# GpSimd's and the transfer queue's orders kept as written in the rounds that make w_down's operands, and these operands asked for behind the last part of x

## The chip, the cores and the metric

The kernel runs on one core of a Trainium2 chip. The core has five engines with an instruction stream each: TensorE (PE in the profile, with its weight loads as PEld), VectorE (DVE), ScalarE (ACT), GpSimd (POOL) and SyncE (SP). SP computes nothing here: it issues every transfer between the device memory and the on-chip buffers, one behind the other, and where a transfer has to wait for something, SP waits, and all that stands behind it waits too. The metric is the device time of one execution in microseconds (us); lower is better.

## The reference

A layer norm feeds two branches that are multiplied at the end: attention with 32 heads of 18 columns, and a gated feed-forward net.

```python
def reference(A_x, A_wqkv, A_wo, B_x, B_w_gate, B_w_up, B_w_down):
    def _A_ref(x, wqkv, wo):
        ...
        scores = jnp.einsum("bhqd,bhkd->bhqk", q, k) * (Dh ** -0.5)
        p = _softmax(scores, axis=-1)
        o = jnp.einsum("bhqk,bhkd->bhqd", p, v)
        return (lambda x, *d: x.transpose(*d))(o, 0, 2, 1, 3).reshape(B, S, D) @ wo
    def _B_ref(x, w_gate, w_up, w_down):
        return (_gelu(x @ w_gate) * (x @ w_up)) @ w_down
    xn = _layernorm(A_x, axis=-1)
    s = _A_ref(xn, A_wqkv, A_wo)
    g = _silu(_B_ref(xn, B_w_gate, B_w_up, B_w_down))
    return A_x + s * g
```

There are 2048 tokens of 576 columns in float32, and the feed-forward net is 4608 wide. Products run in a 22-bit format (`F32R`); so every operand is split into a high and a low part, and three products stand for one.

## The kernel before

**Sections and rounds.** Behind a prologue (layer norm, projections) the work is a row of 144 *sections*. A section takes one block of 512 tokens (there are four, `NB`) and one slab of 128 hidden columns: 27 pairs of matmuls into `pg` and `pu` (gate and up), the activation into a tile `t`, and its split into `ah` and `al`. Two sections make a *round* (`G = 2`): at its end the slab of `w_down` for these 256 columns is there, and the product of the round, "downs" in the code, is added into `Y` on TensorE in the section after, behind its gate-and-up pairs. 18 rounds make a token block. In sections 10 to 137 the attention is woven into the gate-and-up pairs: `pm` is a score product for the row maxima, `pe` one for the exponentials, `acc` the product with the values, which stands at the end of every odd section. One group of four heads and 512 queries (a *unit*, `u`) takes four sections; its maxima have to stand in rows of the tiles `q` (by the way `m2t`, `mT`, `q<-mT`) before its first `pe`.

**The rounds in question.** Rounds 23 to 67 (`SEVEN`) form the product with w_down with seven block products in place of eight. They need sums of blocks of w_down as split operands, `BH` and `BL` (`bh`, `bl` in the profile). These are made once, in the 18 rounds before (`PREP`, rounds 5 to 22, sections 10 to 45), and kept in device memory as `ds` (one tensor a round; the tensor that is made for round 4 of a block is read again for round 4 of the others). In such a round:

- `load_down` (L774) brings the slab of w_down into `TY`; at the round's end it is split into `bh`, `bl` on GpSimd (L119 and L121), where the ordinary product reads it.
- in the first section of the next round `cut_differences` (L713) makes four differences in `TY` (L718), and splits them: the high part goes into a buffer called `raw`, the low part stays in `TY`.
- in the second section of that round `stores` (L722 to L726) writes `ds`: two pieces of `bh`, two of `bl`, all of `raw`, all of `TY`. Only then is `TY` free for the next `load_down`.

The buffer `raw` has two copies (L131). They serve the weights of gate and up of the next section (`load_gu`, L134) and that high part in turn. From `raw` GpSimd makes `wh` and `wl`, three pieces of each in a section (`split_gu`, L142); the pieces of the next section are made while this one runs.

In the rounds of `SEVEN`, `load_seven` (L730) reads `bh` and `bl` back from `ds` at the end of the round's second section. At the end of a token block `load_xd_part` (L150) loads the next block's transposed x in three parts of two tiles (`xd`), and GpSimd copies each to the other 64 partitions.

**What sets the order.** TensorE's order is the order in which the code is written. For the other engines and for SP's queue a scheduler orders the instructions, except where the code calls `tc.keep_in_program_order` on an instruction: these stay in the order of the code among themselves. `kept` (L516) does that only towards the end of the kernel. `no_sync(a, b, why)` puts a behind b in the order without a wait. The functions take a parameter (`keep`, `pin`) that says which of the two holds.

In the attention's loop (the last lines printed below) one turn asks first for the stores of K (`store_k`, `kx<-Km`), then runs a section (weights, `ds` stores and w_down in it), then asks for the next K (`load_k`: `Ks<-kx`, and `Km<-qk` in six pieces), the queries and maxima, and in odd sections the values (`load_v`, `VS`).

Of the kernel before, what the change touches and what calls it, by code (L numbers as in the profile page):

```python
# [17 lines left out]
P = 128  # L18
NT = S // P
TB = 512  # L20
# [60 lines left out]
def kernel(ctx: ExitStack, tc: tile.TileContext, x, wqkv, wo, w_gate, w_up, w_down, out):  # L81
# [36 lines left out]
    def split(hi, lo, raw, keep=lambda i: i):  # L118
# [3 lines left out]
        return first  # L122

    def split_ap(hi, lo, raw):
        tc.keep_in_program_order(nc.scalar.activation(hi, raw, AF.Copy))
        nc.gpsimd.tensor_tensor(lo, raw, f(hi), op=ALU.subtract)
# [22 lines left out]

    def load_xd_part(b, xd, c, keep=lambda i: i):  # L150

        for i in range(2):
            t = wts.tile([P, XG, TB], F32R, name=f"xd{i}_{c}")
            asked[:] = [nc.sync.dma_start(f(t)[0:HR], xhs[b][i, c * HR:(c + XG) * HR, :].rearrange("(k p) t -> p k t", p=HR))]
            keep(nc.gpsimd.tensor_copy(t[HR:P], t[0:HR]))  # L155
            xd[i].append(t)
# [556 lines left out]
    def cut_differences(r, raw):  # L713

        raw = raw.rearrange("p g (c n) -> p (g c) n", c=2)
        b11, b12, b21, b22 = range(4)
        for to, x, y in ((b11, b12, b11), (b12, b22, b12), (b22, b22, b11), (b21, b22, b21)):
            keep(nc.gpsimd.tensor_tensor(raw[:, to], raw[:, x], raw[:, y], op=ALU.subtract))  # L718
        high, low = raw_wide().rearrange("p (s n) -> p s n", s=4).bitcast(F32R), raw.bitcast(F32R)
        split(high, low, raw, keep)  # L720

        def stores():  # L722
            for i, (four, t) in enumerate(((BH, high), (BL, low))):
                nc.sync.dma_start(ds[r][i, :, B11, :], f(four)[:, b11, :])
                nc.sync.dma_start(ds[r][i, :, B21:B22 + 1, :], f(four)[:, b21:b22 + 1, :])
                nc.sync.dma_start(ds[r][i, :, T1:T2 + 1, :], f(t))  # L726

        FF["stores"].append(stores)

    def load_seven(r):  # L730
        for i, t in enumerate((BH, BL)):
            nc.sync.dma_start(f(t), ds[r][i])

# [39 lines left out]

    def load_down(r, raw):  # L774
        kept(nc.sync.dma_start(raw, w_down[r * G * P:(r + 1) * G * P, :].rearrange("(g p) n -> p g n", p=P)))
        return raw

    def section(specials=(), tag="f", raw_d=None, ahead=True):
# [20 lines left out]
        if g == G - 1 and not seven(n):  # L799
            FF["rawd"] = FF.pop("first_d") if n < G else load_down(  # L800
                r, raw_d() if raw_d else down_pair(TY) if n // G in PREP else raw_wide().rearrange("p (g n) -> p g n", g=G)) \
# [17 lines left out]
        def x_part(k):  # L819
            if new_x:  # L820
                load_xd_part(b + 1, xd, XG * k, tc.keep_in_program_order)

# [4 lines left out]
        if nxt and ahead:  # L827
            split_gu(nxt, NG - 1, pin)
        FF["w"] = nxt
# [23 lines left out]
    def finish(pool=ffn, cut=split):  # L853
# [66 lines left out]
    with tc.tile_pool(name="att", bufs=1, reuse_waits="tile") as att:  # L920
# [43 lines left out]

        def load_v(n):

            u, c = divmod(n, NA)
            if u < NU:
                g = u % NQ
                nc.sync.dma_start(VS[n % VB][:, 0:VC * VW].rearrange("p (t x) -> p t x", x=VW),  # L970
                                  vs[c * TB:(c + 1) * TB, QD * g:QD * (g + 1), :].rearrange("(t p) h d -> p t (h d)", p=P))

# [399 lines left out]
```

## Time and profile before

| | |
|---|---|
| time, median of 3 runs (lowest to highest) | 2692.07 us (2683.3 to 2692.53) |
| the profiled execution | 2687.61 us |
| its span, first to last instruction | 2685.8 us |
| mean granted TensorE clock | 0.978 |
| PE busy | 2572.2 us (96%) |
| DVE, POOL, ACT busy | 2072.8, 1724.0, 1578.4 us |
| moved by the queue of SP | 516.74 MB in 456992 packets |
| chain that ended last | PE 78%, POOL 8%, DMA 7%, DVE 3% |

The span is what the trace shows; 1.8 us of the execution lie outside it. "Busy" of PE counts slowly clocked matmuls in full, so 96% does not mean that TensorE could not be faster: a stretch has to be compared with another stretch of the same work. In the 40 slices of the page each slice is 67 us; the rounds of `PREP` lie in slices 5 to 16.

### The profile page before, as it was taken

What the parts mean: (1) busy time and instruction counts of PE and PEld (TensorE: products, weight loads), DVE (VectorE), ACT (ScalarE), POOL (GpSimd) and SP (SyncE); (2) the same over time, 40 slices, a digit from 0 to 9 for tenths busy, and PEclk for the clock granted to TensorE, in tenths of its full rate; (3) what the DMA queues carried; (4) which work ended last, traced back from release to release, by engine and by line L of the source; (5) the groups of instructions that cost most, each with busy time, mean ns of one, the idle gap of its engine ahead of it and who ended that gap; (6) DMA issues with size and microseconds to landing.
All of it is one profiled execution on the core that took longest, in us unless ns stands there. A gap on an engine that the chain in (4) does not pass through costs nothing.

```text
span 2685.8 us, 59575 instructions
## 1 busy us (share of the span) xinstructions
PE 2572.2 (96%) x21766; PEld 1963.5 (73%) x21766; DVE 2072.8 (77%) x3621; ACT 1578.4 (59%) x3009; POOL 1724.0 (64%) x2031
## 2 busy tenths in 40 slices
PE   9999989888988999999999999999999999999999
PEld 8889867575665767777776777777776777777788
DVE  5218867575766767899998899999998999999277
ACT  3223555454555555677776677777666676666722
POOL 3137656555556766666666866666667866666785
PEclk9999999898998999999999999999999999999999
DMA  7877555666667667767668766666768766666584
GB/s 248 276 248 186 153 173 174 183 180 177 188 174 215 204 177 207 195 189 193 187 188 210 207 189 191 192 187 189 194 192 210 205 189 194 191 192 180 142 241 141
DMA packets 457284, 520.55 MB, mean 194 GB/s; under 512 B 117776, under 2 KB 314416, under 8 KB 456992
## 3 DMA queue, kind: packets, MB, share of 16 engines
q1 hardware_dynamic: 456992, 516.74, 67.7%
q8 instruction: 174, 2.85, 0.5%
q14 instruction: 118, 0.97, 0.1%
HBM read 407.95 MB, written 108.64 MB: 192 GB/s over the span
## 4 chain that ended last, share of the span: by engine, by line
PE 78%; POOL 8%; DMA 7%; DVE 3%; issue 2%; SPq 2%; ACT 0%; POOLq 0%; ACTq 0%; DVEq 0%
PE pg L532 24%; PE acc L1083 12%; PE py L670 9%; PE pm L995 8%; PE pe L1048 7%; PE po L194 6%; PE pu L532 5%; PE py L600 4%; PE po L1232 2%; POOL wl L121 2%; DMA ds<-TY 2%; DVE mx L998 1%; POOL TY L718 1%; DMA raw<-in_B_w_up_dram 1%; POOL TY L121 1%
## 5 line engine op out<-in xcount | busy, mean ns | idle before, releaser
L1049 ACT ACTIVATE pT<-pe 128x512 f32<-128x512 f32 x2048 | 1155.8, 599 | 570.3 <-PE pm L995 297.3
L998 DVE TENSOR_REDUCE mx<-pm 128x1 f32<-128x512 f32 x2048 | 1266.9, 682 | 265.8 <-PE pm L995 197.3
L532 PE MATMUL pu<-xd,wh 64*128 64x512 f32 x2592 | 953.0, 400 | 15.1 <-POOL xd L155 14.5
L532 PE MATMUL pg<-xd,wh 64*128 64x512 f32 x2592 | 952.5, 400 | 8.2 <-POOL wh L119 5.0
L1048 PE MATMUL pe<-q,Ks 64*128 64x512 f32 x2048 | 797.4, 398 | 22.1 <-DMA q<-mT 15.3
L995 PE MATMUL pm<-Km,q 64*128 64x512 f32 x2048 | 800.9, 398 | 1.3 <-DVE accs L1088 0.8
L532 PEld LDWEIGHTS pg<-xd,wh 64*128 64x128 f32 x2592 | 489.1, 189 | 139.7 <-POOL ah L119 26.2
L532 PE MATMUL pg<-xd,wl 64*128 64x512 f32 x1296 | 516.5, 399 | 59.3 <-POOL wl L121 59.3
L121 POOL TENSOR_TENSOR wl<-raw,wh 128x384 fp32r<-128x384 f32 x432 | 444.1, 1029 | 176.2 <-PE pu L532 156.6
L532 PE MATMUL pu<-xd,wl 64*128 64x512 f32 x1296 | 516.1, 398 | 0.0
L532 PEld LDWEIGHTS pu<-xd,wh 64*128 64x128 f32 x2592 | 489.6, 189 | 28.3 <-POOL xd L155 17.8
L1083 PE MATMUL acc<-pT,VS 128*32 128x512 f32 x4096 | 452.8, 594 | 0.0
L1048 PEld LDWEIGHTS pe<-q,Ks 64*128 64x128 f32 x2048 | 381.6, 190 | 57.8 <-DMA q<-mT 17.3
L995 PEld LDWEIGHTS pm<-Km,q 64*128 64x128 f32 x2048 | 386.2, 189 | 44.2 <-DVE mx L998 8.7
L119 POOL TENSOR_SCALAR wh<-raw 128x384 fp32r<-128x384 f32 x432 | 231.4, 537 | 249.5 <-DMA raw<-in_B_w_up_dram 183.0
L1083 PEld LDWEIGHTS acc<-pT,VS 128*32 128x32 f32 x4096 | 127.2, 110 | 290.4 <-issue 280.5
L532 PEld LDWEIGHTS pg<-xd,wl 64*128 64x128 f32 x1296 | 245.5, 189 | 105.5 <-POOL wl L121 69.1
L121 POOL TENSOR_TENSOR al<-t,ah 128x512 fp32r<-128x512 f32 x264 | 266.1, 1008 | 21.9
L532 PEld LDWEIGHTS pu<-xd,wl 64*128 64x128 f32 x1296 | 245.4, 189 | 5.1
L670 PE MATMUL py<-bh,ah 128*128 128x288 f32 x630 | 191.3, 304 | 0.5 <-DVE Y L679 0.5
L670 PE MATMUL py<-bl,ah 128*128 128x288 f32 x630 | 186.4, 296 | 0.0
L670 PE MATMUL py<-bh,al 128*128 128x288 f32 x630 | 185.2, 294 | 0.0
(198 smaller groups left out, 3866.5 us busy)
## 6 DMA issues: line engine op xcount, KB each, us to landing
Ks<-kx SPq DMA_DIRECT2D x256, 256.0 KB
Km<-kx SPq DMA_DIRECT2D x192, 256.0 KB
bl<-ds SPq DMA_DIRECT2D x45, 1008.0 KB
bh<-ds SPq DMA_DIRECT2D x45, 1008.0 KB
raw<-in_B_w_gate_dram SPq DMA_DIRECT2D x144, 288.0 KB
raw<-in_B_w_up_dram SPq DMA_DIRECT2D x144, 288.0 KB
VS<-vs SPq DMA_DIRECT2D x128, 152.0 KB
qk<-t SPq DMA_DIRECT2D x72, 256.0 KB
```

The source lines that it names most:

```text
L119: first = nc.gpsimd.tensor_scalar(hi, raw, 1.0, 1.0, op0=ALU.mult, op1=ALU.mult)
L121: low_part[:] = [keep(nc.gpsimd.tensor_tensor(lo, raw, f(hi), op=ALU.subtract))]
L194: nc.tensor.matmul(o, st, m, start=(i == 0), stop=(i == len(TERMS) - 1))
L532: nc.tensor.matmul(o, w[1 + wp][k][rr, c, :], xd[xp][k][rr, c, :], start=(i == 0), stop=(i == len(terms) - 1))
L600: return nc.tensor.matmul(py, hs[g][a][rr, j * P:(j + 1) * P], wd[w][rr, g, 288 * c:288 * c + 288], start=start, stop=stop)
L670: nc.tensor.matmul(py, x[:, a, t * P:(t + 1) * P], y[:, w, :], start=(i == 0), stop=(i == 2))
L995: nc.tensor.matmul(pm, QS[u, r][rr, t * P:(t + 1) * P], keys(KM, u, c, r)[rr, :], start=True, stop=True)
L998: return nc.vector.tensor_reduce(MX[u][:, 2 * r + a, t, c:c + 1], pm, axis=AX.X, op=ALU.max)
L1048: nc.tensor.matmul(pe, keys(KS, u, c, r)[rr, t * P:(t + 1) * P], QS[u, r][rr, :], start=True, stop=True)
L1049: nc.scalar.activation(PT[u, kt][:, 2 * r + a, :], pe, AF.Exp, scale=SCALE)
L1083: nc.tensor.matmul(ACC[u][32 * a:32 * a + 32, :], VS[(u * NA + c) % VB][:, v:v + 32], pt[:, a, :], start=first, stop=last, skip_group_chec ...
L1232: nc.tensor.matmul(po, parts_of(b, j)[x_][:, k, :], OW[w][c][k], start=(i == 0), stop=(i == len(OUT) - 1))
```

## The change

Three things are changed, and nothing in what is computed:

1. In the sections of `PREP` the GpSimd instructions of the weights' splits (`split_gu`), of the hidden values and of w_down's slab (`split_kept`), and on SP the transfers of the weights, of K, of the values, of x, of `ds` and of w_down are kept in the order of the code (`sp_pin`, `pool_pin`).
2. `stores` writes the split differences (`raw`, `TY`) ahead of the pieces of `bh` and `bl`; before, these came first for each of the two parts.
3. `load_seven` puts the loads of `bh` and `bl` behind the last part of x where one was asked for in the same section.

```diff
+    def split_kept(hi, lo, raw):
+        split(hi, lo, raw, tc.keep_in_program_order)
...
-    def load_xd_part(b, xd, c, keep=lambda i: i):
+    def load_xd_part(b, xd, c, keep=lambda i: i, sp_keep=lambda i: i):
...
             asked[:] = [nc.sync.dma_start(f(t)[0:HR], xhs[b][i, c * HR:(c + XG) * HR, :].rearrange("(k p) t -> p k t", p=HR))]
+            sp_keep(asked[0])
...
-        def stores():
-            for i, (four, t) in enumerate(((BH, high), (BL, low))):
-                nc.sync.dma_start(ds[r][i, :, B11, :], f(four)[:, b11, :])
-                nc.sync.dma_start(ds[r][i, :, B21:B22 + 1, :], f(four)[:, b21:b22 + 1, :])
-                nc.sync.dma_start(ds[r][i, :, T1:T2 + 1, :], f(t))
+        def stores(keep):
+            for i, t in enumerate((high, low)):
+                keep(nc.sync.dma_start(ds[r][i, :, T1:T2 + 1, :], f(t)))
+            for i, four in enumerate((BH, BL)):
+                keep(nc.sync.dma_start(ds[r][i, :, B11, :], f(four)[:, b11, :]))
+                keep(nc.sync.dma_start(ds[r][i, :, B21:B22 + 1, :], f(four)[:, b21:b22 + 1, :]))
...
     def load_seven(r):
         for i, t in enumerate((BH, BL)):
-            nc.sync.dma_start(f(t), ds[r][i])
+            one = nc.sync.dma_start(f(t), ds[r][i])
+            if asked:
+                no_sync(one, asked[0], "transposed x first")
...
-        keep = kept
+        sp_pin = tc.keep_in_program_order if n // G in PREP else kept
+        pool_pin = tc.keep_in_program_order if seven(n) or n // G in PREP else kept
+        keep = sp_pin
         if asked:
             xd_last = asked.pop()
             def keep(i):
-                no_sync(i, xd_last, "transposed x first")
+                no_sync(sp_pin(i), xd_last, "transposed x first")
...
-            FF["stores"].pop()()
+            FF["stores"].pop()(sp_pin)
...
-                first = split_gu(nxt, k, pin)
-                if k == 0 and n in ATT and n > ATT.start and not seven(n):
+                first = split_gu(nxt, k, pool_pin)
+                if k == 0 and n in ATT and n > ATT.start and pool_pin is kept:
                     no_sync(first, FF["hl"], "hidden values first")
...
+        if n // G in PREP:
+            cut = split_kept
...
+            sp_pin = tc.keep_in_program_order if FF["n"] // G in PREP else lambda i: i
             for h in range(2 * n + LEAD_K, 2 * n + LEAD_K + 2):
-                store_k(h)
+                store_k(h, sp_pin)
             section([p for s in range(s0, s0 + SLOTS) for p in slot_pairs(s)])
             for h in range(2 * n + KB, 2 * n + KB + 2):
-                load_k(h, KS)
-                load_k(h + LEAD_K, KM)
+                load_k(h, KS, sp_pin)
+                load_k(h + LEAD_K, KM, sp_pin)
...
-                load_v(n + 1)
-                load_v(n + 2)
+                load_v(n + 1, sp_pin)
+                load_v(n + 2, sp_pin)
```

The orders of TensorE, VectorE and ScalarE are the same before and after; those of GpSimd and SP differ, as follows.

GpSimd in section 25, the second of its round, before (`t_8020` and `t_8353` hold the hidden values of sections 24 and 25, `wh` and `wl` are the split weights of section 26):

```order
L121 TENSOR_TENSOR al<-t_8020,ah 128x512
L119 TENSOR_SCALAR wh<-raw 128x384
L119 TENSOR_SCALAR bh<-TY 128x1152
L121 TENSOR_TENSOR bl<-TY,bh 128x1152
L121 TENSOR_TENSOR wl<-raw,wh 128x384
L119 TENSOR_SCALAR wh<-raw 128x384
L888 TENSOR_TENSOR num<-num,rb 72x256
L121 TENSOR_TENSOR wl<-raw,wh 128x384
L119 TENSOR_SCALAR wh<-raw 128x384
L121 TENSOR_TENSOR wl<-raw,wh 128x384
L119 TENSOR_SCALAR ah<-t_8353 128x512
L121 TENSOR_TENSOR al<-t_8353,ah 128x512
```

The same place with the change:

```order
L121 TENSOR_TENSOR al<-t_8020,ah 128x512
L119 TENSOR_SCALAR wh<-raw 128x384
L121 TENSOR_TENSOR wl<-raw,wh 128x384
L119 TENSOR_SCALAR wh<-raw 128x384
L121 TENSOR_TENSOR wl<-raw,wh 128x384
L119 TENSOR_SCALAR wh<-raw 128x384
L121 TENSOR_TENSOR wl<-raw,wh 128x384
L119 TENSOR_SCALAR ah<-t_8353 128x512
L121 TENSOR_TENSOR al<-t_8353,ah 128x512
L119 TENSOR_SCALAR bh<-TY 128x1152
L121 TENSOR_TENSOR bl<-TY,bh 128x1152
L899 TENSOR_TENSOR num<-num,rb 72x256
```

The split of w_down's slab (`bh`, `bl`) has moved from between the first `wh` and its `wl` to behind the section's hidden values.

SP's queue in section 27, also the second of its round, before (`ds_125` is the tensor that this round writes, `q_8964` are queries of a later unit):

```order
L139 DMA raw<-in_B_w_gate_dram 64x9x128
L139 DMA raw<-in_B_w_up_dram 64x9x128
L724 DMA ds_125<-bh 128x288
L725 DMA ds_125<-bh 128x576
L726 DMA ds_125<-raw 128x1152
L724 DMA ds_125<-bl 128x288
L725 DMA ds_125<-bl 128x576
L726 DMA ds_125<-TY 128x1152
L985 DMA q_8964<-qk 18x512 x3
L775 DMA TY<-in_B_w_down_dram 128x2x576
```

The same place with the change:

```order
L142 DMA raw<-in_B_w_gate_dram 64x9x128
L142 DMA raw<-in_B_w_up_dram 64x9x128
L728 DMA ds_125<-raw 128x1152
L728 DMA ds_125<-TY 128x1152
L730 DMA ds_125<-bh 128x288
L731 DMA ds_125<-bh 128x576
L730 DMA ds_125<-bl 128x288
L731 DMA ds_125<-bl 128x576
L782 DMA TY<-in_B_w_down_dram 128x2x576
L950 DMA Ks<-kx_109 128x512
```

`ds<-TY`, for which `TY<-in_B_w_down_dram` waits, is the second of the six stores and no longer the last, and the queries stand in part ahead of the weights and in part behind the next K.

SP's queue in section 71, the last of a token block, before (`xd` is the next block's x, `ds_130` holds the operands of the round that ends here):

```order
L732 DMA bl<-ds_130 128x2016
L732 DMA bh<-ds_130 128x2016
L154 DMA xd_0_20877<-xhs_134 64x3x512
L154 DMA xd_0_20880<-xhs_134 64x3x512
L939 DMA Ks<-kx_112 128x512
L939 DMA Km<-kx_105 128x512
L154 DMA xd_3_20942<-xhs_134 64x3x512
L154 DMA xd_3_20945<-xhs_134 64x3x512
L154 DMA xd_6_21000<-xhs_134 64x3x512
L154 DMA xd_6_21003<-xhs_134 64x3x512
L939 DMA Ks<-kx_112 128x512
```

The same place with the change:

```order
L157 DMA xd_0_20877<-xhs_134 64x3x512
L157 DMA xd_0_20880<-xhs_134 64x3x512
L950 DMA Ks<-kx_112 128x512
L950 DMA Km<-kx_105 128x512
L157 DMA xd_3_20942<-xhs_134 64x3x512
L157 DMA xd_3_20945<-xhs_134 64x3x512
L157 DMA xd_6_21000<-xhs_134 64x3x512
L157 DMA xd_6_21003<-xhs_134 64x3x512
L737 DMA bh<-ds_130 128x2016
L737 DMA bl<-ds_130 128x2016
L950 DMA Ks<-kx_112 128x512
```

The two loads of w_down's operands have moved from ahead of the six parts of x to behind them; section 107 has the same. In the other rounds of `SEVEN`, from the second on, the queue's order is what it was.

More of the change, by code (lines that the diff above doesn't have):

```diff
@@ L772, in down, with load_down @@
                     add_down(b, r, py, j, c)
-    def load_down(r, raw):
-        kept(nc.sync.dma_start(raw, w_down[r * G * P:(r + 1) * G * P, :].rearrange("(g p) n -> p g n", p=P)))
+    def load_down(r, raw, keep=None):
+        (keep or kept)(nc.sync.dma_start(raw, w_down[r * G * P:(r + 1) * G * P, :].rearrange("(g p) n -> p g n", p=P)))
         return raw
@@ L797, in section @@
         if g == G - 1 and FF["stores"]:
-            FF["stores"].pop()()
+            FF["stores"].pop()(sp_pin)
         if g == G - 1 and not seven(n):
             FF["rawd"] = FF.pop("first_d") if n < G else load_down(
-                r, raw_d() if raw_d else down_pair(TY) if n // G in PREP else raw_wide().rearrange("p (g n) -> p g n", g=G)) \
+                r, raw_d() if raw_d else down_pair(TY) if n // G in PREP else raw_wide().rearrange("p (g n) -> p g n", g=G), sp_pin) \
                 if ahead else FF.pop("next_d")
@@ L820, in x_part @@
             if new_x:
-                load_xd_part(b + 1, xd, XG * k, tc.keep_in_program_order)
+                load_xd_part(b + 1, xd, XG * k, tc.keep_in_program_order, sp_pin)
         for k in range(NG - 1):
@@ L827, in section @@
         if nxt and ahead:
-            split_gu(nxt, NG - 1, pin)
+            split_gu(nxt, NG - 1, pool_pin)
         FF["w"] = nxt
@@ L963, in keys, with load_v @@
             return ring[:, (2 * (u * NA + c) + r) % KB, :]
-        def load_v(n):
+        def load_v(n, keep=lambda i: i):
             u, c = divmod(n, NA)
```

4 lines of the change are left out of this document (2 added, 2 removed).

## The prediction

> **What bounds the kernel now.** I read the page's head first: the change is judged against a span of this length, and the profiled execution is 1.8 us longer (2687.61 us).
>
> ```profile
> span 2685.8 us, 59575 instructions
> ```
>
> Then I cut the trace into its 144 sections, at every 27th pair of matmuls into `pg` and `pu`, and took stretches of whole sections into the view by windows (stretch, its length, busy time of PE, PEld, DVE, ACT and POOL with instruction counts, granted clock, DMA share, GB/s).
>
> ```profile
> 341.20:374.40 33.20, 33.20 (x339) 26.08 (x336) 28.20 (x48) 22.42 (x44) 16.98 (x18) 1.00 0.64 187
> 592.50:678.90 86.40, 72.78 (x669) 55.26 (x667) 56.34 (x99) 45.81 (x89) 48.29 (x50) 0.92 0.61 176
> 857.00:1029.70 172.70, 159.86 (x1480) 121.22 (x1480) 126.88 (x215) 101.28 (x197) 117.58 (x118) 0.95 0.66 191
> 1431.30:1447.00 15.70, 15.70 (x134) 13.54 (x130) 15.15 (x28) 11.94 (x23) 14.26 (x19) 1.00 0.58 163
> 1464.00:1489.50 25.50, 19.66 (x132) 15.41 (x128) 16.41 (x31) 12.65 (x24) 22.81 (x27) 0.87 0.82 164
> 2065.30:2087.80 22.50, 18.22 (x134) 14.87 (x130) 15.58 (x31) 12.75 (x24) 21.02 (x24) 0.92 0.86 174
> ```
>
> The first row is sections 13 and 14, where PE never waits: 33.2 us for two sections of `PREP`, 66.4 for the four of an attention unit, which I call a **turn**. The second is one turn later, sections 25 to 28: 86.4 us, so 20 lost. The third is sections 37 to 45, nine sections at 76.8 a turn. The fourth is an even section of `SEVEN` without a stall (15.7), the last two are sections 72 and 108, the first of token blocks 2 and 3: together 48.0 where 31.4 would do. No engine is full in the slow turn. In it PE's granted clock is 0.92, in the stretches without a stall 1.00.
>
> Third view, PE's waits in sections 15 to 45 (total, times, longest):
>
> ```profile
> PE pg L532 <- POOL wl L121: 59.3, 22, 7.3
> PE pe L1048 <- DMA q<-mT: 15.3, 8, 4.3
> ```
>
> PE waits for the low part of the weights, on GpSimd. Why GpSimd is late, the chain of waits in the slow turn shows (start, length, what):
>
> ```profile
> 603.38 5.70 DMA ds<-TY
> 609.10 3.77 DMA TY<-in_B_w_down_dram
> 613.07 1.12 POOL bh L119
> 614.27 1.72 POOL bl L121
> ...
> 616.84 1.00 POOL wl L121
> 617.89 0.79 PE pg L532
> ```
>
> The row of 616.84 is behind that of 614.27 on one engine: `wl` stands behind `bl` on GpSimd, `bl` behind w_down's landing, that behind the store of `TY`. Last, SP's timeline and GpSimd's, for what closes the circle (start, length of the issue; x6 is six in a row):
>
> ```profile
> 345.82 0.61 SPq L139 DMA_DIRECT2D raw<-in_B_w_gate_dram  x1
> ...
> 581.83 0.61 SPq L139 DMA_DIRECT2D raw<-in_B_w_gate_dram  x1
> ...
> 601.09 0.61 SPq L139 DMA_DIRECT2D raw<-in_B_w_gate_dram  x1
> ...
> 609.10 0.39 SPq L775 DMA_DIRECT2D TY<-in_B_w_down_dram  x1
> ...
> 619.93 0.39 SPq L939 DMA_DIRECT2D Ks<-kx  x1
> 620.37 2.13 SPq L948 DMA_DIRECT2D Km<-qk  x6
> ...
> 626.45 0.35 SPq L954 DMA_DIRECT2D kx<-Km  x1
> 626.84 0.68 SPq L139 DMA_DIRECT2D raw<-in_B_w_gate_dram  x1
> ...
> 644.46 0.63 SPq L139 DMA_DIRECT2D raw<-in_B_w_gate_dram  x1
> ...
> 650.15 0.44 SPq L726 DMA_DIRECT2D ds<-TY  x1
> ...
> 655.57 0.41 SPq L775 DMA_DIRECT2D TY<-in_B_w_down_dram  x1
> ...
> 668.82 1.04 SPq L954 DMA_DIRECT2D kx<-Km  x2
> 669.91 0.62 SPq L139 DMA_DIRECT2D raw<-in_B_w_gate_dram  x1
> ...
> 772.99 0.61 SPq L139 DMA_DIRECT2D raw<-in_B_w_gate_dram  x1
> ```
>
> The four distances between requests for weights make one turn: 581.83 to 601.09 is 19.3, to 626.84 is 25.7, to 644.46 is 17.6, to 669.91 is 25.5; 88.1 in all. From 345.82 to 772.99 lie five turns: 85.4 each. The two long legs hold a request for w_down: 8.0 us after the weights in one (609.10), 11.1 in the other (655.57), then 17.7 and 14.3 until the next weights. In these tails **SP hardly pauses**: the 16 rows from 609.10 to 626.45 last 15.0 of 17.7 us, the 18 from 655.57 to 668.82 13.2 of 14.3. The two short legs end when GpSimd has read the last piece of `raw`:
>
> ```profile
> 592.29 0.81 POOL L718 TENSOR_TENSOR TY<-TY 128x288 f32<-128x288 f32 x1
> ...
> 600.06 1.00 POOL L121 TENSOR_TENSOR wl<-raw,wh 128x384 fp32r<-128x384 f32 x1
> ```
>
> The differences stand ahead of that last `wl` (592.29 to 600.06, then the weights at 601.09). So I take the turn to be set by a circle of SP's queue, transfers and GpSimd, with PE a follower.
>
> **The change, part by part.**
>
> *GpSimd's order.* Nothing is added or removed. `bh`/`bl` (1.12 and 2.61, which end at 616.84) stand behind the weights and hidden values. So `wl` no longer waits for w_down, some 6 us per long leg. Their reader, the product of the round, starts at the end of the following section, some 10 us on; that hides the move. Without this cover the cost would be the 3.7 us of the two splits, once a round. But the circle doesn't shrink by 6: behind that wait come SP's tails. What SP's queue gains is what I count.
>
> *Store order and SP's order.* `ds<-TY` stands second of six. From the weights: 0.6 and 0.6 for two requests, 0.4 for `ds<-raw`, 0.4 for `ds<-TY`, then its landing (5.7 in the first leg by the chain; 655.57 − 650.15 = 5.4 in the second): 7.5 to 8.2, taken as 8.0. In the first leg this is the 8.0 of before, since there the scheduler had put three of the stores ahead; in the second it is 3.1 less than 11.1. The four stores of `bh` and `bl` take SP's time inside that landing; were the landing short, they would cost 1.6 to 2.7 us (four times 0.39 to 0.68, the rows of single requests). In the first tail I take out the wait for `rT`, since the changed order asks for `rT` ahead of the weights, and for its reader `rb` behind w_down:
>
> ```profile
> SPq L878 <- DMA rT<-sums: 1.6, 1, 1.6
> ```
>
> That is 17.7 to 16.1. The second tail gets 0.2 more, half a request, since one for `kx` moves into some of the tails. Legs after: 19.3 + 24.1 + 17.6 + 22.5 = 83.5, which is 4.6 under this turn's 88.1. In the other four turns some of the stores and queries already lay differently. The gain of a turn then lies between 2.9 (the second leg's 3.1 less 0.2) and 4.6; I take 3.5, between the two since neither end has more rows for it. Five turns: **−17.5 us**. The bounds are wide: if 11.1 were to stay in both legs, a turn would be about 3 longer (+15 in all); if the pinned order also took the pauses out of the tails (2.7 and 1.1) and half of GpSimd's differences out of the short leg (7.8 from 592.29 to 600.06), 7.7 more would go (−56).
>
> A rule speaks against counting on the queue at all. The Trainium skill, "DMA: Bandwidth & Descriptors", section "Issuing engines are not separate DMA queues", says that the time the issuing engine spends on starting a transfer is usually small relative to the transfer. By it the queue wouldn't bind, PE would follow the splits, and the rival A below would come. The trace disagrees here: seven requests (619.93 and 620.37) held SP for 2.6 us, and the tails are full of such rows.
>
> *Sections 35 and 36* hold the first xd change, inside `PREP`. There is no w_down operand to move there; weights and w_down go ahead or behind x by a transfer or two. I count 0, between −6 and +6: one landing of `ds<-TY` (5.4 to 5.7) more or less ahead of a part of x.
>
> *Sections 37 to 45*, 2.25 turns at 76.8: K comes in one request there rather than six, so SP is less full, and a turn is already 8.6 shorter. The second leg's 2.9 is what remains to be saved: 2.25 × 2.9, **−6.5 us**; ends 0 and −23.3 (172.7 − 4.5 × 33.2).
>
> *w_down's operands behind x*, sections 71 and 107:
>
> ```profile
> 1446.96 0.34 SPq L732 DMA_DIRECT2D bl<-ds  x1
> ...
> 1450.05 1.31 SPq L154 DMA_DIRECT2D xd<-xhs  x2
> ...
> 1459.06 1.46 POOL L155 CAST xd<-xd 64x1536 fp32r<-64x1536 f32 x1 [7.86 <-DMA xd<-xhs]
> ...
> 1476.80 1.46 POOL L155 CAST xd<-xd 64x1536 fp32r<-64x1536 f32 x1
> ...
> 1478.32 0.79 PE L532 MATMUL pu<-xd,wh 64*128 64x512 f32 x1 [3.20 <-POOL xd L155]
> ...
> 1483.30 0.61 PE L670 MATMUL py<-bh,ah 128*128 128x288 f32 x1
> ...
> 822.28 0.59 SPq L154 DMA_DIRECT2D xd<-xhs  x1
> ...
> 827.50 1.46 POOL L155 CAST xd<-xd 64x1536 fp32r<-64x1536 f32 x1 [4.64 <-DMA xd<-xhs]
> ```
>
> With `bl` and `bh` ahead, x is copied 9.0 us after its request; in section 35, without them, 5.2. That is 3.8 per part and up to 3.1 more for the earlier request (1446.96 to 1450.05), against a stall that ends at 1478.32. What is late next is `bh` and `bl`: 2 MB asked for last, wanted by the product (1483.30 now, some 10 us into a section that runs freely). Everything asked for from 1446.96 had landed by 1476.80. If the same bytes take the same time, the product starts at 1477, about 6 earlier; if they are quicker, the section becomes 15.7. I take 6 per section: **−12 us**; ends −6 (one of the two only) and −16.6 (48.0 − 31.4).
>
> *Sections 46 to 48*: the handover to `SEVEN` with the scheduler free again. 0, within 4 either way: one stall of the longest kind that `q<-mT` shows, 4.3.
>
> **Sum.** −17.5 − 6.5 − 12 = −36, from the profiled execution's 2687.61: **2651.6, say 2652 us**. That execution lies 4.5 under the median of 2692.07, inside the runs' 2683.3 to 2692.53, so against the median I expect about 1.4% less.
>
> **The rivals.**
>
> *A, PE takes over.* If the tails are full only because SP catches up after each wait, they shrink with the waits, and `PREP` runs at PE's pace: 5 × (85.4 − 66.4) = 95, and 23.3 and 16.6: 2687.6 − 135 = **2553**. For it: the wait for `wl` is the largest and goes. Against it: the tails' rows themselves, and `q<-mT`, already the second wait. Chance 0.10. This is how it would go by the sentence of the Trainium skill, "DMA: Bandwidth & Descriptors", named above.
>
> *B, the stall only moves.* PE waits at `q<-mT` or at the weights for as long as it did at `wl`, since the queue's length is unchanged; only x gains: 2687.6 − 12 = **2676**, 2669 to 2685 with the small terms. For it: the queue has the same requests in each turn, and the second leg saves only if `ds<-TY` lands as quickly in a bunch of six stores. Chance 0.20.
>
> *C, slower.* All that SP asks for in an odd section now stands behind w_down's request in written order, and that waits for `ds<-TY`: K, values, maxima, the next weights. Let x be the time from the weights to w_down's request in both long legs. At 8 a turn saves 3.5; each microsecond more costs two a turn. 7.25 turns of 2(x − 8) − 3.5, less the 12 of x: even at x = 10.6, and slower by over 13.5 us from x = 11.5. At 12.5 it gives **2716**. For it: the scheduler had put other work into that wait, and 11.1 has been seen. Against it: that 11.1 had all six stores ahead. Chance 0.12.
>
> That the orders aren't what the code says is excluded by the rows shown with the change.
>
> **How the numbers follow.** My forecast has 0.58, with its own range 2610 to 2686 (the distances to the bounds above, added as squares since they are separate: 42 down, 34 up). A and C reach beyond on either side; 2592 to 2687 leaves out most of both, some 2 in 10. About 0.5%, 13.5 us, is what a measurement of this kernel can tell from no change. Faster by more: forecast, A, and nearly half of B: 0.77. Within: the rest of B and the middle of C, 0.13. Slower: 0.10.
>
> **What would show it.** PE's wait for `wl` in sections 15 to 45 falls from 59.3 to under 15, and the one for `q<-mT` grows. The request for w_down follows the weights by 8 us in both long legs, and a turn is near 82. Sections 72 and 108 have no wait for `xd`, and are 16 to 20 us long. The forecast is wrong if the turn goes below 75 (the queue didn't bind: A), stays at 85 (B), if w_down is asked for 11 us behind the weights (C), or if the product in section 72 waits for `bh` as long as PE waited for x.

## The result, and the profile after

The changed kernel takes 2706.82 us (median of 5 runs, 2705.46 to 2712.64) against 2692.07: ratio 1.0066, 95% interval 1.0047 to 1.0086. It is slower by two thirds of a per cent, where about 1.4% less was forecast. The head of the page, and sections 13 and 14, 25 to 28, 37 to 45, 72 and 108 in the view by windows:

```profile
span 2705.0 us, 59524 instructions
```

```profile
342.20:382.80 40.60, 37.04 (x338) 27.35 (x336) 29.30 (x51) 22.15 (x44) 19.48 (x22) 0.92 0.66 195
602.40:690.90 88.50, 71.29 (x664) 54.93 (x664) 56.50 (x98) 45.40 (x89) 49.55 (x50) 0.94 0.62 175
879.50:1054.60 175.10, 159.30 (x1484) 121.63 (x1481) 126.40 (x219) 101.37 (x197) 115.20 (x117) 0.96 0.63 186
1486.60:1508.70 22.10, 18.90 (x132) 15.40 (x128) 15.60 (x31) 12.86 (x24) 17.92 (x22) 0.85 0.92 239
2084.50:2104.00 19.50, 16.31 (x132) 13.59 (x128) 15.06 (x31) 12.63 (x24) 15.85 (x19) 1.00 0.98 268
```

Section by section against before, the span's 19.2 us are: sections 10 to 14 +9.8 (of these 13 and 14 +7.4, first row), 15 to 34 +13.9, 35 and 36 +0.2, 37 to 45 +2.4, 46 to 48 −2.4, 72 and 108 −6.3, the rest +1.6. PE's waits in sections 15 to 45 of the changed kernel (total, times, longest):

```profile
PE pe L1059 <- DMA q<-mT: 44.8, 6, 9.2
PE pg L536 <- POOL wh L119: 27.6, 10, 6.1
...
PE pg L536 <- POOL wl L121: 8.1, 11, 1.0
```

The 59.3 us at `wl` became 8.1, as meant. PE now stands at `q<-mT` (15.3 before) and at `wh`, whose weights come late. SP's timeline over a turn, and then GpSimd's, of the changed kernel:

```profile
702.50 0.67 SPq L142 DMA_DIRECT2D raw<-in_B_w_gate_dram  x1
...
710.80 0.38 SPq L782 DMA_DIRECT2D TY<-in_B_w_down_dram  x1
711.31 0.67 SPq L950 DMA_DIRECT2D Ks<-kx  x1
...
716.21 0.35 SPq L950 DMA_DIRECT2D Ks<-kx  x1
...
727.32 0.68 SPq L142 DMA_DIRECT2D raw<-in_B_w_gate_dram  x1
...
747.00 0.65 SPq L142 DMA_DIRECT2D raw<-in_B_w_gate_dram  x1
...
755.22 0.39 SPq L782 DMA_DIRECT2D TY<-in_B_w_down_dram  x1
...
771.59 0.61 SPq L142 DMA_DIRECT2D raw<-in_B_w_gate_dram  x1
...
790.65 0.67 SPq L142 DMA_DIRECT2D raw<-in_B_w_gate_dram  x1
```

```profile
733.90 0.51 POOL L119 TENSOR_SCALAR wh<-raw 128x384 fp32r<-128x384 f32 x1 [11.21 <-DMA raw<-in_B_w_up_dram]
...
737.49 3.47 POOL L722 TENSOR_TENSOR TY<-TY 128x288 f32<-128x288 f32 x4
...
742.28 2.68 POOL L121 TENSOR_TENSOR TY<-TY,raw 128x1152 fp32r<-128x1152 f32 x1
...
745.97 1.00 POOL L121 TENSOR_TENSOR wl<-raw,wh 128x384 fp32r<-128x384 f32 x1
```

The legs here are 24.8, 19.7, 24.6 and 19.1 us. w_down is asked for 8.3 and 8.2 us behind the weights, but the tails behind it are 16.5 and 16.4. The short leg 727.32 to 747.00 still ends with the last `wl`, behind the differences and their split. From the weights of section 18 to those of section 34 a turn lasts 89.3 us, before 86.0; below, "turn" is that number. What SP waits for between 500 and 800 us, first before, then after:

```profile
SPq L726 <- POOL raw L119: 22.4, 4, 5.8
SPq L775 <- DMA ds<-TY: 19.4, 7, 3.9
SPq L139 <- POOL ah L119: 12.3, 4, 5.8
SPq L139 <- POOL num L888: 4.9, 1, 4.9
SPq L948 <- DMA raw<-in_B_w_gate_dram: 4.6, 6, 1.5
SPq L948 <- DMA TY<-in_B_w_down_dram: 3.6, 3, 1.8
SPq L1112 <- DMA raw<-in_B_w_up_dram: 3.5, 3, 1.3
SPq L954 <- DMA raw<-in_B_w_up_dram: 2.5, 2, 1.3
...
SPq L948 <- DMA raw<-in_B_w_up_dram: 1.6, 2, 1.0
```

```profile
SPq L142 <- POOL ah L119: 18.1, 4, 5.5
SPq L142 <- POOL wl L121: 16.2, 3, 5.8
SPq L959 <- DMA raw<-in_B_w_gate_dram: 8.3, 6, 2.9
SPq L950 <- DMA raw<-in_B_w_up_dram: 8.0, 7, 1.3
SPq L782 <- DMA ds<-TY: 7.8, 6, 1.5
SPq L996 <- DMA TY<-in_B_w_down_dram: 5.8, 3, 3.1
SPq L950 <- DMA TY<-in_B_w_down_dram: 4.9, 3, 1.9
```

The wait for `ds<-TY` fell by 11.6 us. The waits for landings of weights and slab, in requests that need neither (K or queries are asked for, and SP stands at `TY` or `raw`), rose from 15.8 to 27.0, by 11.2: **what the early request gained is paid again at the next landings.** And GpSimd holds SP for 34.3 us; before it was 39.6, more than half of it at the store of `raw`. Neither kernel gets past that. A kernel with all of the change but the new order of the stores (e_oldstores below) shows the same trade without the other parts: between the same times it waits 17.0 us for `ds<-TY`, 20.5 for those landings and 31.3 for GpSimd, and its turn is 89.3 too. So of the 9.2 us that the early request takes off the first, 6.5 come back at the landings and 3.0 at GpSimd.

### The profile page after: what moved, and what is told of

Read it like the earlier page. It is cut to its first block, busy times and chain, and to the rows that moved or that the text cites. A ratio compares the mean times of both kernels' runs of the same rounds, so it can differ in the third digit from the quotient of the medians.

```text
span 2705.0 us, 59524 instructions
## 1 busy us (share of the span) xinstructions
PE 2568.3 (95%) x21766; PEld 1956.5 (72%) x21766; DVE 2070.0 (77%) x3621; ACT 1575.9 (58%) x3009; POOL 1725.3 (64%) x2031
## 4 chain that ended last, share of the span: by engine, by line
PE 81%; DMA 7%; POOL 6%; SPq 2%; DVE 1%; issue 1%; ACT 0%; POOLq 0%; DVEq 0%; ACTq 0%
PE pg L536 25%; PE acc L1094 14%; PE py L674 9%; PE pm L1006 8%; PE pe L1059 8%; PE po L198 6%; PE pu L536 4%; PE py L604 4%; PE po L1244 2%; DMA raw<-in_B_w_up_dram 2%; DMA ds<-TY 2%; DMA Ks<-kx 2%; POOL wl L121 2%; POOL TY L121 1%; POOL TY L722 1%
## 5 line engine op out<-in xcount | busy, mean ns | idle before, releaser
L536 PEld LDWEIGHTS pu<-xd,wh 64*128 64x128 f32 x2592 | 487.5, 188 | 25.0 <-POOL xd L159 16.8
L536 PEld LDWEIGHTS pg<-xd,wl 64*128 64x128 f32 x1296 | 244.6, 189 | 53.6 <-POOL wl L121 16.4
```

The costliest lines, as they stand in the source:

```text
L536: nc.tensor.matmul(o, w[1 + wp][k][rr, c, :], xd[xp][k][rr, c, :], start=(i == 0), stop=(i == len(terms) - 1))
```

## The experiments

Three questions, 18 kernels. "Before" was run beside each group and is 2689.04 to 2693.35 us there; ratios are to it. Times are medians. h_k4 and x_quarter leave out a part of the operands.

| kernel | us | ratio (95%) | turn, us |
|---|---|---|---|
| before / changed | 2692.07 / 2706.82 | 1.0066 (1.0047, 1.0086) | 86.0 / 89.3 |
| e_pool | 2695.28 | 1.0011 (1.0000, 1.0023) | 85.7 |
| e_sp | 2661.11 | 0.9889 (0.9871, 0.9907) | 80.4 |
| e_stores | 2694.24 | 1.0008 (0.9993, 1.0023) | 84.9 |
| e_x | 2681.82 | 0.9969 (0.9958, 0.9980) | 86.0 |
| e_nopool | 2649.17 | 0.9830 (0.9814, 0.9847) | 79.7 |
| e_oldstores | 2715.30 | 1.0079 (1.0063, 1.0094) | 89.3 |
| f_last | 2634.08 | 0.9773 (0.9757, 0.9789) | 80.2 |
| f_last_old | 2641.97 | 0.9809 (0.9791, 0.9827) | 81.4 |
| f_nosp | 2633.22 | 0.9773 (0.9758, 0.9789) | 79.0 |
| h_k4 | 2613.75 | 0.9707 (0.9692, 0.9721) | 76.7 |
| x_quarter | 2612.99 | 0.9711 (0.9692, 0.9730) | 76.9 |
| a_kfirst | 2697.23 | 1.0029 (1.0015, 1.0043) | 86.4 |
| i_kfirst_f | 2627.65 | 0.9770 (0.9752, 0.9788) | 78.8 |
| i_kfirst | 2640.84 | 0.9822 (0.9801, 0.9844) | 79.3 |
| g_q_first | 2628.56 | 0.9756 (0.9730, 0.9782) | 80.0 |
| g_q_mid | 2618.48 | 0.9723 (0.9709, 0.9737) | 78.7 |
| y_two | 2631.93 | 0.9785 (0.9760, 0.9809) | 79.8 |
| y_two_q | 2614.70 | 0.9721 (0.9699, 0.9742) | 78.3 |

### Which part costs: one part alone

Each of these kernels has one part of the change and is otherwise the kernel before. **e_pool:**

```diff
+        pool_pin = tc.keep_in_program_order if seven(n) or n // G in PREP else kept
...
+        if n // G in PREP:
+            cut = split_kept
```

> Of the change only GpSimd's pinned order in the rounds of PREP; SP's queue is left to the scheduler, the stores and the loads of bh and bl are as before. Theory 1 (the pin on SP's queue lengthens the turn; GpSimd's order alone lets wl go ahead of w_down): faster than before by 10 to 30 us, the wait of PE for wl in sections 15 to 45 under 20 us, a turn of 80 to 84 us. Theory 2 (GpSimd's pinned order is what costs: the last piece of wl comes behind the differences and the hidden values, so the weights' buffer is free 2 us later in one leg): slower by 10 to 20 us, a turn of 88 to 90 us.

2695.28 us, no change within the interval: neither theory. GpSimd's order alone moves PE's waits and leaves the turn (85.7).

**e_sp:**

```diff
+        sp_pin = tc.keep_in_program_order if n // G in PREP else kept
...
+            sp_pin = tc.keep_in_program_order if FF["n"] // G in PREP else lambda i: i
```

> Of the change only SP's pinned order in the rounds of PREP, with the six stores in their old order among themselves; GpSimd's order is left to the scheduler. Theory 1: slower than before by 20 to 40 us, more than the whole change, since w_down is asked for some 11 us behind the weights in both long legs and everything in the queue waits behind it; a turn of 90 us or more. Theory 2: within 10 us of before, a turn of 84 to 87 us.

2661.11 us, **30 less** than before: outside of both. SP's pin, which theory 1 blamed, helps when it stands alone. In this kernel the scheduler has put a part of the differences, and all of their split, behind the last `wl`. GpSimd, then SP, at the end of a short leg of e_sp:

```profile
623.37 1.03 POOL L121 TENSOR_TENSOR wl<-raw,wh 128x384 fp32r<-128x384 f32 x1
624.35 1.70 POOL L722 TENSOR_TENSOR TY<-TY 128x288 f32<-128x288 f32 x2
626.14 1.16 POOL L119 TENSOR_SCALAR raw<-TY 128x1152 fp32r<-128x1152 f32 x1
```

```profile
625.49 0.43 SPq L960 DMA_DIRECT2D kx<-Km  x1
626.01 0.65 SPq L142 DMA_DIRECT2D raw<-in_B_w_gate_dram  x1
```

The last `wl` is over at 624.40, and SP comes to the weights at 626.01 without a wait. In the last three turns the short legs are 13.4 to 16.8 us there (19 and 20 in the changed kernel), the long ones 24.6 to 26.3. e_sp also shows where sections 10 to 14 lose: section 14 is 24.1 us there, with PE at `q<-mT` for 4.4, and 16.2 in e_pool. That loss belongs to SP's pin.

**e_stores** (the six stores in the new order) and **e_x** (`bh`, `bl` behind x):

```diff
+            for i, t in enumerate((high, low)):
+                keep(nc.sync.dma_start(ds[r][i, :, T1:T2 + 1, :], f(t)))
+            for i, four in enumerate((BH, BL)):
...
+            if asked:
+                no_sync(one, asked[0], "transposed x first")
```

> Of the change only the order in which the six stores are written in the code; no pins. Both theories: within 8 us of before, either way; the scheduler may move the stores apart as it did. If the distance from the weights to w_down's request falls to 8 us in both long legs, faster by 5 to 8 us.

> Of the change only the loads of bh and bl behind the last part of x, in sections 71 and 107. Both theories: 6 us less than before (sections 72 and 108 at 22.1 and 19.5 us as in the changed kernel, 25.5 and 22.4 before), which the measurement cannot tell from no change; the trace shows it. If the order of these loads had nothing to do with it, sections 72 and 108 stay at 25 and 22 us.

e_stores is unchanged in time, as both theories had it. But the second sentence of what was expected missed: w_down is asked for 6.7 to 8.3 us behind the weights there in both long legs of the last three turns, and 5 to 8 us less didn't come. The second long leg is 1.4 us shorter than before on average (23.7), the first 0.4 longer (24.9). e_x saves 0.31%, with sections 72 and 108 at 21.8 and 20.4 us, about as expected.

### Why the parts together lose what one of them gains

> The change without GpSimd's pinned order in PREP (SP's pins, the new order of the stores, bh and bl behind x). Theory A (SP's pin alone took 30 us off; GpSimd's pin, with SP's, gives them back because the four differences and their split, 7.4 us, then all stand ahead of the last wl, and SP can ask for the next weights only behind it): 2645 to 2665 us, short legs of 13 to 16 us. Theory B (the new order of the stores is what spoils SP's pin): 2690 us or more.

2649.17 us. Taking GpSimd's pin out of the change (the edit of e_pool undone) saves 58 us of 2706.82; with SP left to the scheduler the same pin cost 4 or nothing. The new order of the stores isn't to blame (theory B falls). **e_oldstores** is the change with the loop of `stores` as it was before:

> The change with the stores in their old order (ds<-TY the last of six). Theory A: w_down is asked for 10.5 to 11 us behind the weights in place of 8.3, twice a turn, so slower than the change by 10 to 30 us: 2717 to 2737 us. Theory B: faster than the change by 20 us or more.

2715.30 us: 8.5 slower than the change, less than expected, and not in the turn (sections 35 to 45 hold it). w_down is asked for 10.4 to 11.5 us behind the weights there, 8.2 to 8.6 in the change, and the turn is 89.3 in both. The tails behind w_down's request are 14.7 and 13.8 us in its last three turns, in the change 17.2 and 16.0: what is saved ahead of the request comes back behind it. So the early request, on which the forecast rested, gains nothing in the turn.

**f_last** has all of the change, and the call that makes the differences further down in `section`:

```diff
-            if k == 1 and g == 0 and FF["later"]:
-                FF["later"].pop()()
...
             split_gu(nxt, NG - 1, pool_pin)
+        if g == 0 and FF["later"]:
+            FF["later"].pop()()
```

> The change with the differences moved, in GpSimd's pinned order, from between the second and the third piece of the weights to behind the third; all else as changed. Theory A: SP asks for the weights as soon as its queue comes to them, 3.7 and 5.9 us earlier in the two short legs, while ds<-TY waits some 1.7 us longer for the differences in the two long legs: a turn of 82 to 84 us in place of 89, 2665 to 2680 us. Theory B: within 10 us of the change (2697 to 2717).

2634.08 us, 73 less than the change and 59 less than before, more than theory A expected. GpSimd and SP at the end of a short leg of f_last:

```profile
699.25 1.01 POOL L121 TENSOR_TENSOR wl<-raw,wh 128x384 fp32r<-128x384 f32 x1
700.22 3.48 POOL L722 TENSOR_TENSOR TY<-TY 128x288 f32<-128x288 f32 x4
```

```profile
701.32 0.93 SPq L965 DMA_DIRECT2D kx<-Km  x2
702.35 0.65 SPq L142 DMA_DIRECT2D raw<-in_B_w_gate_dram  x1
```

The same six instructions (four differences and the two of their split) stand on the other side of the last `wl`, and the short legs are 14.1 and 14.9 us. The long legs are 25.7 and 25.4 (25.7 and 24.7 in the change). Sections 37 to 45 take 156.0 us (175.1 in the change).

> The kernel before this one (f_last) with the old order of the stores: bh and bl can be stored while the differences are still made, ds<-TY then goes some 1 us later than there. Theory A: within 10 us of f_last. Theory B: faster than f_last by 20 us or more.

> f_last without the pins on SP's queue: GpSimd's pinned order with the differences behind the last piece of the weights, the new order of the stores, bh and bl behind x. Theory A (the place of the differences is what counts): 2630 to 2665 us. If SP's pin is what makes it fast, and GpSimd's place only undoes the harm: 2680 to 2700 us, as with GpSimd's pin alone.

f_last_old: 2641.97, 8 slower than f_last, within the 10 of theory A. f_nosp: 2633.22, the same as f_last. So with the differences out of the way SP's pins bring nothing and cost nothing; what e_sp gained fits with the place that the scheduler gave the differences there, not with SP's order. Against the change, the place of the differences is the whole gain of 73; of the 59 against before, `bh` and `bl` behind x bring a part (e_x saved 9.5).

### What sets a long leg

**h_k4** is f_last with `for n_, i in enumerate((0, 1)):` in `load_k` in place of `(0, 1, 0)`, so it leaves out the second copy of K's high part:

> f_last with two of the three rows' blocks of each half of K left out (the second copy of its high part isn't loaded: Km in four requests a pair in place of six, so part of the scores' operand is wrong; all products run as before). Theory C (the long legs last 25 us whatever else because of the number of requests that SP has to get through, each request standing behind the landing of an earlier one): the legs with 12 requests of Km lose a third of these, long legs of 22 to 23.5 us, short ones of 13 to 14, a turn of 72 to 76 in place of 80, 2595 to 2620 us. Theory D (a long leg is set by the landing of w_down's stores and slab and by PE): legs and time as in f_last, 2625 to 2642 us.

2613.75 us, a time that theory C named, but not by its way: the long legs are 24.3 and 24.9, not 22 to 23.5. 16 requests fewer a turn shorten it by 3.5 us (80.2 to 76.7), 0.2 us each. The Trainium skill's sentence in "DMA: Bandwidth & Descriptors", section "Issuing engines are not separate DMA queues", that the time to start a transfer is usually small relative to it, would let one expect less; here the requests count, though they aren't all. Their bytes went with them, so this run doesn't part the two. The trace suggests a reason why the long legs kept most of their length: SP stands at the stores, until GpSimd has made the differences, for 27.3 us between 500 and 800 us, in f_last for 20.6.

**g_q_first** and **g_q_mid** are f_last with

```diff
-                at(n + 1, 0, max_rows, um - 1)
+                at(n + 1, 1, max_rows, um - 1, tc.keep_in_program_order if (FF["n"] + 1) // G in PREP else lambda i: i)
```

and `tasks(n, 1)` ahead of `store_k` (first) or just behind `section` (mid); `max_rows` pins its requests with the last argument.

> f_last with the eight requests q<-mT pinned too, ahead of the weights of the same turn of the loop in place of behind w_down and K. Theory C (SP's queue sets the turn, and PE's wait of 8 us at q<-mT is only where PE meets it): that wait shrinks and another takes its place, a turn of 78 to 81 us, within 12 us of f_last. Theory D (PE waits for the landing itself, so the maxima's way sets the turn): the 42 us of this wait go, a turn of 70 to 74, 2590 to 2610 us.

> f_last with the eight requests q<-mT pinned between w_down's request and the loads of K. Theory C: within 12 us of f_last. Theory D: half of the gain of the run with them ahead of the weights, 2605 to 2625 us.

2628.56 and 2618.48 us. g_q_mid's is 15.6 under f_last, outside of theory C's 12 and inside D's range. The wait at `q<-mT` all but goes from PE's list in both (1.0 us is left in g_q_mid), and in its place PE waits for `wh` (39.1 us in sections 15 to 45 of g_q_mid, f_last 7.5). The turn stays at 80.0 and 78.7: theory C as to the turn and to the wait that takes the other's place. g_q_mid's gain of 16 is 6 in sections 10 to 14 and 6 in 15 to 34.

**x_quarter** is f_last with a quarter of the slab; it leaves the other columns of w_down out:

```diff
+        if keep == tc.keep_in_program_order and r != PREP[0]:
+            keep(nc.sync.dma_start(raw[:, :, 0:144], w_down[r * G * P:(r + 1) * G * P, 0:144].rearrange("(g p) n -> p g n", p=P)))
+            return raw
```

> f_last with a quarter of the columns of w_down's slab loaded in the rounds of PREP after the first (the other columns keep what the buffer held, so the product is wrong there; all other work is as before). Theory E (in a long leg SP stands first at the landing of ds<-TY, then, a few requests on, at the landing of the slab, 5.6 us after its request; an earlier request gives back there what it gained): the long legs fall from 25.5 to 22.5 to 23.5, a turn from 80 to 75 to 77, 2600 to 2622 us. Theory F (the long leg is set by the sum of the requests, or by PE through K's ring): long legs of 25 and 2625 to 2642 us.

2612.99 us and a turn of 76.9, as theory E; the long legs are 23.9 and 23.1 (25.7 and 25.4), the first a little over its 22.5 to 23.5. SP's waits at the slab's landing between 500 and 800 us fell from 12.5 us in f_last to 0.2. So this landing is a part of the long leg, 2 us of it; whether the bytes that went too have a share isn't parted here.

**a_kfirst**, **i_kfirst_f** and **i_kfirst** are the change, f_last and g_q_mid with w_down's request put off until K has been asked for:

```diff
+        if g == G - 1 and n // G in PREP and ahead and n >= G:
+            FF["slab"] = lambda: load_down(r, down_pair(TY), sp_pin)
-        if g == G - 1 and not seven(n):
+        elif g == G - 1 and not seven(n):
...
                 load_k(h + LEAD_K, KM, sp_pin)
+            if "slab" in FF:
+                FF["rawd"] = FF.pop("slab")()
```

> The change with w_down's request behind the 14 requests for K that followed it; the differences stay ahead of the last piece of the weights. Theory E: K's requests go out while ds<-TY lands, w_down is asked for some 13 to 14 us behind the weights, 5 us later than in the change, and the long legs are shorter all the same, by 2 to 3 us each; the short legs stay at 19 and 20: a turn of 84 to 86 in place of 89, 2670 to 2690 us. Theory F: long legs of 25, time as the change, 2700 to 2715 us.

> f_last with w_down's request behind the 14 requests for K. Theory E: long legs of 22.5 to 23.5, short ones of 14 to 15 as in f_last, a turn of 74 to 77, 2600 to 2620 us, unless the slab's split then comes too late for the product of the round (PE would wait for bl at the end of the even sections). Theory F: 2625 to 2642 us.

> g_q_mid (the maxima's requests pinned ahead of K) with w_down's request behind K. Theory E: a turn of 72 to 76, 2585 to 2610 us, the fastest of all. Theory F: 2610 to 2625 us, as g_q_mid.

a_kfirst: w_down is asked for 14.3 to 15.6 us behind the weights, **6 us later** than in the change, and the long legs are shorter, 23.9 and 23.6, the time 2697.23, between the theories. i_kfirst_f: long legs of 24.3 and 24.6, 2627.65, by its ratio no gain over f_last, as theory F had it. i_kfirst lost, outside of both theories: 2640.84, 22 more than g_q_mid. Its wait is at the product, as PE's waits in sections 15 to 45 of i_kfirst show:

```profile
PE py L604 <- POOL bl L121: 31.4, 14, 2.9
PE py L604 <- POOL bh L119: 13.8, 8, 2.6
```

That is the cover that the prediction named for `bh` and `bl`: it holds for a request at 8 us, not for one at 16 to 21; a_kfirst has 18.9 us of the same two waits.

**y_two** and **y_two_q** (f_last and g_q_mid) bring the slab in turn into `TY` and into four places of `Y` that these rounds don't use, so that its request needn't wait for `ds<-TY`:

```diff
-                r, raw_d() if raw_d else down_pair(TY) if n // G in PREP else ...
+                r, raw_d() if raw_d else (down_pair(TY) if n // G % 2 else Y[:, :, 4:6, :].rearrange("p g c n -> p g (c n)")) if n // G in PREP else ...
```

> f_last with w_down's slab brought in turn into TY and into four free places of Y, so that its request has no landing of ds<-TY to wait for (nothing is left out). Theory E (the long leg is two landings one behind the other, of ds<-TY and of the slab): w_down is asked for 5 to 7 us behind the weights, long legs of 20.5 to 23, a turn of 71 to 76, 2590 to 2615 us. Theory F (SP has to stand at some landing all the same, since each of its requests waits for an earlier one): long legs of 24 to 26, 2620 to 2640 us.

> y_two with the maxima's requests q<-mT pinned between w_down's request and K, as in g_q_mid. Theory E: 2580 to 2605 us, the fastest. Theory F: 2610 to 2625 us, as g_q_mid.

2631.93 us against f_last's 2634.08, 2614.70 against g_q_mid's 2618.48: theory F by their times, and by their ratios no clear gain. SP's waits between 500 and 800 us in y_two:

```profile
SPq L951 <- DMA raw<-in_B_w_up_dram: 9.6, 7, 2.5
...
SPq L960 <- DMA raw<-in_B_w_gate_dram: 8.3, 7, 2.3
SPq L951 <- DMA Y<-in_B_w_down_dram: 6.9, 4, 2.2
SPq L997 <- DMA TY<-in_B_w_down_dram: 5.0, 3, 2.0
```

w_down's request itself no longer waits for `ds<-TY`, and the long legs are 25.7 and 24.9 all the same: the four rows of landings make 29.8 us now (28.2 for the same landings in f_last). But theory E's condition wasn't met: w_down is asked for 8.0 us behind the weights on average, after 9.0 in f_last, and not 5 to 7, since SP stands at the stores ahead of it until GpSimd has made the differences (21.0 us between 500 and 800, in f_last 20.6). So y_two doesn't exclude E. **What fixes the long leg at 23 to 26 us in nearly every kernel is not settled.** Of single causes, the slab's landing gave 2 us a leg, K's requests up to 1.4, w_down's place up to 1.8, the wait for `ds<-TY` nothing that can be told. GpSimd's part, by the stores that wait for the differences, was not tested alone.

The fastest kernels that leave nothing out, y_two_q and g_q_mid, beat both the kernel before (by 2.8%) and the changed one.

## Why the prediction was wrong

- *The circle of SP's queue, transfers and GpSimd sets the turn, PE follows*: right. PE's wait for `wl` went, and came back as a wait for `q<-mT` and `wh`; in g_q_mid and i_kfirst it moved twice more with the turn near 79.
- *w_down is asked for 8.0 us behind the weights in both long legs*: right, 8.2 to 8.6 in the last three turns.
- **The failed step: "Legs after: 19.3 + 24.1 + 17.6 + 22.5", the two long legs in it.** It took the tails as SP's own time, which an earlier start would leave as it is (16.1 and 14.5). In the last three turns the four legs are 25.6, 20.1, 24.3 and 19.0 in the order of the first tail, and before they were 24.5, 17.7, 25.1 and 19.0. Against the prediction's sum of 83.5 that is 1.5 and 1.8 more in the long legs, 2.5 more and 0.3 less in the short ones. The tails are 17.2 and 16.0 us on average (before 16.8 and 14.2), and SP stands in them at landings for 2.3 and 2.4 us (before 0.8 and 1.2). The rows that were read as SP's own time held such pauses already: the one of 658.34, four requests in 2.26 us, has 0.9 us at w_down's landing in it. e_oldstores settles that the early request is worth nothing in the turn (89.3 with and without it), e_stores agrees, and x_quarter shows a part of what it runs into.
- **The short legs, taken as unchanged (19.3 and 17.6).** That GpSimd holds them was right, and the range allowed for half of the differences to leave them. I did not look at what the pinned order makes of them. All four differences, the split and a `wh` now stand ahead of the last `wl`: 737.49 to 745.97. This leg, 17.7 on average before, is 20.1. Moving that call takes 4 to 6 us off each short leg, the largest lever found (f_last).
- *Sections 37 to 45, −6.5*: +2.4. What failed here is the step of the short legs: f_last, with the differences behind the last `wl`, takes 156.0. The price of the early request was about right in these sections: with the old order of the stores they take 181.0 in e_oldstores (the change 175.1) and 163.9 in f_last_old (f_last 156.0). These are single profiles, and before and e_x, which are alike up to section 71, differ by 3.1; but both pairs differ by some 8 us in their medians as well.
- *x ahead of `bh` and `bl`, −12*: a size. Sections 72 and 108 gained 6.3 together, at the lower end given. In the changed kernel (SP, GpSimd, GpSimd, PE, PE):

```profile
1472.66 1.28 SPq L157 DMA_DIRECT2D xd<-xhs  x2
```

```profile
1477.36 1.46 POOL L159 CAST xd<-xd 64x1536 fp32r<-64x1536 f32 x1 [3.56 <-DMA xd<-xhs]
...
1496.16 1.46 POOL L159 CAST xd<-xd 64x1536 fp32r<-64x1536 f32 x1
```

```profile
1497.67 0.79 PE L536 MATMUL pu<-xd,wh 64*128 64x512 f32 x1 [3.20 <-POOL xd L159]
...
1502.65 0.61 PE L674 MATMUL py<-bh,ah 128*128 128x288 f32 x1
```

  The first part of x is copied 4.7 us after its request (5.2 was the estimate, 9.0 before). But PE's wait for `xd`, which was to go, is still 3.2 us in each of the two sections, and section 72 lasts 22.1 and not 16 to 20. The last copy stands on GpSimd without a wait for a transfer, 9.6 us into section 72 and not 12.8: 3.2 less, and PE's last wait is for it. I had read that wait as one for the landing.
- *Not counted: sections 10 to 14, +9.8.* The prediction began at section 15, since 13 and 14 ran without a stall. SP's pin put `q<-mT` behind w_down and K there (e_sp +9.8, e_pool +1.8 for these sections).
- *Rival C, slower*, was nearest in its sign, but not by its price: it needed w_down's request at 11.5 us or more, and it came at 8.3. Rival B had the stall right, that it moves to `q<-mT` and to the weights (59.3 and 15.3 us at `wl` and `q<-mT` before; 8.1, 44.8 and 27.6 at `wl`, `q<-mT` and `wh` after), but not the turn, which it left at 85. Rival A is excluded: PE's pace of 66.4 was reached by none of the kernels.

## What to carry to other kernels

Where an engine holds a buffer for a transfer, look at what stands between the first and the last reader of that buffer; six instructions, put behind the last reader rather than ahead of it, were worth 73 us of 2707. A pin that cost 4 us or nothing alone cost 58 beside another, so the parts of such a change are worth measuring singly. An order that is fixed by hand fixes everything that the scheduler had mixed, so each queue is to be read through anew. And a stretch of back-to-back issues isn't yet that queue's own time: ask, with one wait removed, at which landing it stops next.

## What was not expected of the hardware

SP's requests wait for landings that they don't need. In the changed kernel w_down is asked for at 710.80; one request for `Ks` and six for `Km` follow, and the next `Ks` goes out at 716.21, after 1.5 us at w_down's landing. The same shows behind the weights (in the list of waits of the changed kernel the rows of L959, `Km<-qk`, and L950, `Ks<-kx`, on `raw`). In both places it is the eighth request behind the transfer that waits. The semaphores in the traces show why: SP's requests announce their landings on eight semaphores in turn, and nearly every request (2868 of 3035 in the changed kernel) waits for its own, which the request eight before it has to set first. Waits for the landing of the request eight before add up to 187.8 us over the whole changed kernel and to 155.1 before. So this is an order that the program brings along, and what more semaphores would do was not tested.
